# Reordering the start of a one-core RWKV-plus-MLP kernel: the columns' step ahead of zeroing, k turned ahead of r, and VectorE's early steps and four loads in another order

## The chip, the cores and the metric

The kernel runs on one core of one Trainium2 chip. A core has five engines with a queue of instructions each: TensorE (PE in the profile, with its weight loads as PEld), VectorE (DVE), ScalarE (ACT), GpSimd (POOL) and SyncE (SP). Each engine takes its queue strictly in order, and engines wait for one another with semaphores. The metric is the device time of one execution in microseconds (us); less is better. Before the change it is 168.96 us, the median of 3 runs (168.95 to 168.97).

## The reference

A linear-attention layer with a decaying state is followed by a two-layer MLP with a leaky ReLU. There are 4 batches, 8 heads, 768 tokens and a head size of 48, so the MLP sees 3072 tokens of 384 features.

```
B, H, S, D = r.shape                      # 4, 8, 768, 48
state = np.zeros((B, H, D, D))
for t in range(S):
    cur = einsum('bhd,bhe->bhde', u[None] * kt, vt)
    y[:, :, t] = einsum('bhd,bhde->bhe', rt, state + cur)
    state = w[None, :, :, None] * state + einsum('bhd,bhe->bhde', kt, vt)
x = y.transpose(0, 2, 1, 3).reshape(B * S, H * D)      # 3072 x 384
h = x @ w_in                              # 384 x 2048
out = np.maximum(0.01 * h, h) @ w_out     # 2048 x 384
```

## The kernel before

The 3072 tokens are cut into 24 stages of 128 tokens. Stage n handles batch n mod 4 and the 128-token chunk n div 4, so stages 0 to 3 are the first chunk of the four batches and carry no state; from stage 4 on a state from four stages earlier is read.

Each stage goes through the same steps, and each step has a short name. The string ORDER near the top of the file lists these names; a small scheduler walks the list, records each step on its engine, derives the waits from what is read and written, and plays the five queues. The place of a name in ORDER therefore sets the order within an engine's queue and, for TensorE, which PSUM bank a step takes; names of different engines that stand side by side do not hold one another up unless one needs the other's result. The names that matter here, with the line that issues the instructions:

- Loads, all issued by GpSimd except the first k (ScalarE's queue) and the first r and the small vectors (SyncE's queue): `k5`, `r4`, `v1` are one stage's k, r or v (L241, or L232 for stage 0); `wi0` to `wi3` are quarters of w_in (L251), `wo0` to `wo3` quarters of w_out (L255); `w8` (L706), `u8` (L707), `w` (L703) and `u` (L708) are copies of the vectors w and u.
- Constants on VectorE: `ones` (L278), `one` (L709), `qk0` (six memsets, L319), `v0z` and `v0y` (zero the gaps of v, L310), `wlz` (L322, L323), `zr` (L314, L315), `id8` (a small identity, L302), `id` (identity, L294), `tri` (mask, L298), `exps` (L306). GpSimd makes `tcol` (L268) and `trow` (L273), token numbers.
- The columns of decays: `Cw` on TensorE (L542) needs `w8`, `id8` and `zr`; `Wl` (L561) takes its logarithm on ScalarE, and `E` (four activations, L354) makes the table of decays by token with which stage 0 is scaled. `bc` on TensorE (L335) spreads w over 128 rows; `lnw` (L342), `qtab` and `ktab` (L349) make the tables for the other stages on ScalarE. `u16`, `U`, `utab` (L363, L367, L372) spread u. `wu8`, `Cu`, `C` (L359, L553, L568) make columns of w times u.
- Stage 0's operands: `c0q@` and `c0k@` cast r and k on VectorE (L438); `T0q` and `T0k` turn them on TensorE (L453); `t0q` and `t0k` scale them out of PSUM on VectorE (L466).
- Other early stages: `P1q`, `P1k` scale r and k by a table on VectorE (L390); `T1q`, `T1k` turn them on TensorE (L453); `t1q`, `t1k` copy them out on ScalarE (L471). From stage 6 a DMA turns them instead (`X6T`, L395).
- `A` multiplies the turned tiles into 128x128 scores on TensorE (L482); `M0a`, `M0b` mask one half each on VectorE (L491, from stage 4 L495). For stages 0 to 3 the diagonal comes from `X` on VectorE (product of the turned tiles, L405), `D` on TensorE (L510) and `Q` on VectorE (v scaled by it, L412). From stage 4 on it comes from `q` on VectorE (three instructions, L419, L421, L423) and `Q` on GpSimd, which writes two diagonal tiles (L430) into the buffers that `M` then fills in.
- `Y` forms the attention output on TensorE (L614 for stages 0 to 3, L621), `y` copies it to xT on ScalarE (L635). `K` forms k-times-v on TensorE (L523), `S` the next state on VectorE (L586, later L589 and L591); `W` (L576) is the table of decays for the states.
- The MLP: `G` and `J` are blocks of the first matmul (L660) and `g` and `j` their leaky ReLU on ScalarE (L671); `H` is the second matmul (L684), `h` its copy and the store (L696, L698).
- `F9` means nine matmuls of ones times ones whose result nobody reads (L288).

TensorE starts with small work that waits for loads and constants. From some 14 us on it has MLP blocks of the first stages between the attention steps, and after the first 22 us it runs to the end with next to no idle time.

Of the kernel before, what the change touches and what calls it, by code (L numbers as in the profile page):

```python
# [26 lines left out]
ORDER = """
w8 qk0 k0 v0z one r0 trow ones v0y tcol wlz r1 id8 F9 wi1 u8 zr table Cw Wl id E w bc lnw c0q@ T0q c0k@ tri u exps k1
T0k u16 wu8 Cu t0q t0k qtab P1q F6 k3 v3 U A0 ktab T1q v0 t1q X0 C D0 P1k T1k t1k F4 M0b P3k M0a T3k K3 utab X1 A1 D1
Q0 Y0 t3k P0k r3 P3q M1a T3q r2 P2q y0 k2 K0 M1b v1 Q1 W G0.1 Y1 t3q X3 wi3 A3 y1 g0.1 S3 T2q D3 G1.1 g1.1 k5 t2q r5 r4  # L30
P2k T2k wi2 S0 v2 M3b t2k Q3 G0.3 g0.3 G1.3 k4 M3a Y3 P5k A2 y3 P4q T4q v4 wi0 T5k v5 wo3 t4q g1.3 G3.1 q5 t5k Q5 G3.3
g3.3 P5q r6 wo2 X2 g3.1 M2b D2 wo1 G3.2 Q2 G0.2 g0.2 T5q t5q K2 P4k T4k M2a t4k S2 G1.2 g3.2 q4 Q4 K1 S1 Y2 A5 A4 G1.0
y2 G2.1 M5a G0.0 G2.3 M4a M5b Y5 g0.0 y5 M4b Y4 y4 G2.2 g2.2 K4 J2.4 j2.4 k6 wo0 J2.1 J2.2 g1.0 g1.2 S4 k7 P6q q6 j2.1
P6k P7k G2.0 r7 q7 X6T J2.6 j2.6 J2.3 j2.3 k8 G3.0 J2.7 j2.7 k9 r9 j2.2 J2.5 P7q g3.0 g2.3 X7T J2.0 H1 h1 r8 q8 g2.0 Q6
P9k j2.0 P8k H0 j2.5 H3 Q7 A6 P9q X9T P8q X8T v6 A7 M6a v7 M7a g2.1 H2 h2 v9 v11 v10 M6b Y6 M7b y6 Q8 q9 Y7 y7 K5 r11
K6 S6 r10 k10 S5 Q9 v8 K7 S7 h0 h3 k11 J3.0 j3.0 J3.1 j3.1 J3.2 j3.2 J3.3 j3.3 J3.4 j3.4 J3.5 j3.5 J3.6 j3.6 J3.7 j3.7
A8 A9 M8a M8b M9a M9b P10q P10k X10T P11q P11k X11T k12 r12 v12 k13 r13 v13 q10 Q10 q11 Q11 H4 h4 Y8 Y9 y8 y9 K8 K9 S8
S9 H5 h5 J4.0 j4.0 J4.1 j4.1 J4.2 j4.2 J4.3 j4.3 J4.4 j4.4 J4.5 j4.5 J4.6 j4.6 J4.7 j4.7 A10 A11 M10a M10b M11a M11b
P12q P12k X12T P13q P13k X13T k14 r14 v14 k15 r15 v15 q12 Q12 q13 Q13 H6 h6 Y10 Y11 y10 y11 K10 K11 S10 S11 H7 h7 J5.0
j5.0 J5.1 j5.1 J5.2 j5.2 J5.3 j5.3 J5.4 j5.4 J5.5 j5.5 J5.6 j5.6 J5.7 j5.7 A12 A13 M12a M12b M13a M13b P14q P14k X14T  # L40
P15q P15k X15T k16 r16 v16 k17 r17 v17 q14 Q14 q15 Q15 H8 h8 Y12 Y13 y12 y13 K12 K13 S12 S13 H9 h9 J6.0 j6.0 J6.1 j6.1
J6.2 j6.2 P16q P16k X16T P17q P17k X17T A14 A15 J6.3 j6.3 M14a M14b M15a M15b k18 r18 v18 k19 r19 v19 J6.4 j6.4 J6.5
j6.5 J6.6 j6.6 J6.7 j6.7 q16 Q16 q17 Q17 H10 h10 Y14 Y15 y14 y15 K14 K15 S14 S15 H11 h11 J7.0 j7.0 J7.1 j7.1 J7.2 j7.2
P18q P18k X18T P19q P19k X19T A16 A17 J7.3 j7.3 M16a M16b M17a M17b k20 r20 v20 k21 r21 v21 J7.4 j7.4 J7.5 j7.5 J7.6
j7.6 J7.7 j7.7 q18 Q18 q19 Q19 H12 h12 Y16 Y17 y16 y17 K16 K17 S16 S17 H13 h13 J8.0 j8.0 J8.1 j8.1 J8.2 j8.2 P20q P20k
X20T P21q P21k X21T A18 A19 J8.3 j8.3 M18a M18b M19a M19b k22 r22 v22 k23 r23 v23 J8.4 j8.4 J8.5 j8.5 J8.6 j8.6 J8.7
j8.7 q20 Q20 q21 Q21 H14 h14 Y18 Y19 y18 y19 K18 K19 S18 S19 H15 h15 J9.0 j9.0 J9.1 j9.1 J9.2 j9.2 P22q P22k X22T P23q
P23k X23T A20 A21 J9.3 j9.3 M20a M20b M21a M21b J9.4 j9.4 J9.5 j9.5 J9.6 j9.6 J9.7 j9.7 q22 Q22 q23 Q23 H16 h16 Y20 Y21
y20 y21 H17 h17 J10.0 j10.0 J10.1 j10.1 J10.2 j10.2 A22 A23 J10.3 j10.3 M22a M22b M23a M23b J10.4 j10.4 J10.5 j10.5
J10.6 j10.6 J10.7 j10.7 H18 h18 Y22 Y23 y22 y23 H19 h19 J11.0 j11.0 J11.1 j11.1 J11.2 j11.2 J11.3 j11.3 J11.4 j11.4  # L50
J11.5 j11.5 J11.6 j11.6 J11.7 j11.7 H20 h20 H21 h21 H22 h22
"""


# [750 lines left out]
```

## Time and profile before

| what | value |
|---|---|
| median of 3 runs | 168.96 us |
| the profiled execution's own time | 168.68 us |
| its span, first to last instruction | 166.8 us |
| TensorE busy | 160.2 us, 96% of the span |
| VectorE, ScalarE, GpSimd busy | 107.6, 89.0, 111.0 us |

The profile is of one execution. Its times are counted from the first instruction of the span, so some 1.8 us of the execution's own time lie outside it. In the timeline a row gives the start, the duration in us, the engine, the line, the operation and the tiles written and read; several instructions of a kind in a row are merged, and a bracket at the end gives the idle time before the row and what ended it. TensorE's matmuls overlap, so the pace of a series is read from the start of one to the start of the next.

### The profile page before, as it was taken

To read this page: it belongs to the slowest core of one execution; us is meant where nothing else is said; L and a number is where in the kernel's file an instruction comes from. 1 tells how busy PE (TensorE), PEld (TensorE's weight loads), DVE (VectorE), ACT (ScalarE), POOL (GpSimd) and SP (SyncE) were. 2 spreads that over 40 slices of the span, in tenths; PEclk is the share of its full clock that TensorE was granted. 3 is DMA by queue.
4 is the path that set the end of the run, shared out by engine and by line. 5 is a ranking of instruction groups with operands and counts; after the bars stand their busy time and mean duration, and the time that the engine had idled before them with its cause. 6 is when DMAs were issued, how large, how long until landed. Compare 5 with 4: busy or idle time off the path is not lost.

```text
span 166.8 us, 4840 instructions
## 1 busy us (share of the span) xinstructions
PE 160.2 (96%) x2076; PEld 120.6 (72%) x2076; DVE 107.6 (64%) x224; ACT 89.0 (53%) x168; POOL 111.0 (67%) x125
## 2 busy tenths in 40 slices
...
GB/s 109 156 140 157 169 193 192 171 149 173 93 168 220 113 157 130 105 108 155 105 146 118 152 127 127 156 140 140 154 51 165 12 47 51 0 47 51 35 59 96
DMA packets 101267, 20.18 MB, mean 121 GB/s; under 512 B 94459, under 2 KB 101246, under 8 KB 101246
## 3 DMA queue, kind: packets, MB, share of 16 engines
...
q10 hardware_dynamic: 1040, 0.20, 0.6%
q14 instruction: 5, 0.04, 0.1%
HBM read 20.45 MB, written 4.72 MB: 151 GB/s over the span
## 4 chain that ended last, share of the span: by engine, by line
PE 86%; POOL 7%; DMA 3%; DVE 2%; issue 0%; ACT 0%; POOLq 0%
PE ps L684 38%; PE ps L660 36%; PE ps L621 6%; DMA r_sb<-in_r_dram 3%; PE ps L482 3%; PE ps L523 2%; POOL r_sb L241 2%; POOL k_sb L241 2%; POOL v_sb L241 2%; POOL w_in_sb L251 1%; DVE prod L405 1%; DVE s_tok L423 0%; PE ps L453 0%; POOL trow L273 0%; DVE rku L421 0%
## 5 line engine op out<-in xcount | busy, mean ns | idle before, releaser
L660 PE MATMUL ps<-xT,w_in_sb 128*128 128x256 bf16 (+1 forms) x672 | 67.2, 257 | 0.0
L684 PE MATMUL ps<-w_out_sb,gT 128*128 128x384 bf16 (+2 forms) x400 | 65.6, 320 | 0.0
L671 ACT ACTIVATE gT<-ps 128x512 bf16<-128x512 f32 x96 | 56.3, 598 | 13.8 <-PE ps L660 9.7
L660 PEld LDWEIGHTS ps<-xT,w_in_sb 128*128 128x128 bf16 x672 | 57.1, 98 | 7.5 <-DVE sum_t L589 0.5
L430 POOL TENSOR_TENSOR at<-ident,s_tok 128x512 bf16<-128x512 bf16 x40 | 42.7, 1096 | 23.4 <-DVE s_tok L423 23.4
L684 PEld LDWEIGHTS ps<-w_out_sb,gT 128*128 128x128 bf16 x400 | 37.7, 98 | 22.4
L696 ACT ACTIVATE out_sb<-ps 128x384 f32<-128x384 f32 (+2 forms) x25 | 11.8, 477 | 54.5 <-PE ps L684 54.5
L495 DVE CAST_PREDICATED at<-mask,ps 128x512 bf16<-128x512 uint16 x40 | 24.9, 684 | 21.3 <-PE ps L482 21.2
L241 POOL DMA_DIRECT2D v_sb<-in_v_dram x24 | 22.1, 927 | 0.0
L241 POOL DMA_DIRECT2D k_sb<-in_k_dram x23 | 21.2, 925 | 0.0
L241 POOL DMA_DIRECT2D r_sb<-in_r_dram x23 | 21.1, 924 | 0.1
L421 DVE TENSOR_TENSOR rku<-r_sb,ku 128x384 bf16<-128x384 bf16 x20 | 13.8, 688 | 1.1 <-DMA r_sb<-in_r_dram 0.5
L589 DVE TENSOR_TENSOR sum_t<-ps,st 128x384 bf16<-128x384 f32 x16 | 8.8, 550 | 5.6 <-PE ps L523 5.6
L635 ACT ACTIVATE xT<-ps 128x384 bf16<-128x384 f32 x24 | 10.8, 490 | 2.6 <-PE ps L621 2.6
L423 DVE TENSOR_REDUCE s_tok<-rku 128x8 f32<-128x384 bf16 x20 | 11.1, 553 | 0.7
L591 DVE TENSOR_TENSOR st<-sum_t,wl 128x384 bf16<-128x384 bf16 x16 | 10.6, 664 | 0.6
L621 PE MATMUL ps<-at,v_sb 128*32 128x128 bf16 x384 | 10.8, 223 | 0.0
L390 DVE TENSOR_TENSOR qk<-k_sb,ktab 128x384 bf16<-128x384 bf16 x23 | 10.1, 444 | 1.1 <-DMA k_sb<-in_k_dram 1.1
L621 PEld LDWEIGHTS ps<-tp,st 128*32 128x32 bf16 x240 | 7.3, 96 | 3.0 <-issue 1.6
L621 PEld LDWEIGHTS ps<-at,v_sb 128*32 128x32 bf16 x384 | 8.8, 98 | 0.5 <-issue 0.2
L621 PE MATMUL ps<-tp,st 128*32 128x128 bf16 x240 | 9.1, 221 | 0.0
L390 DVE TENSOR_TENSOR qk<-r_sb,qtab 128x384 bf16<-128x384 bf16 x23 | 8.8, 386 | 0.2 <-DMA r_sb<-in_r_dram 0.2
...
## 6 DMA issues: line engine op xcount, KB each, us to landing
...
tp<-qk SPq DMA_TRANSPOSE x18, 5.3
...
```

Source lines behind the costliest of these rows:

```text
L241: add("pool", lambda: G.dma_start(dst, src), R=pace, W=[(which, n)], dma=f"{which}{n}")
L390: add("dve", lambda: V.tensor_tensor(qk[iq][:, H * half:H * half + H, 0:D], hd(src), hd(tab[:, :]), ALU.mult), R=[(name, n), "qk"[half] + ...
L421: add("dve", lambda: V.tensor_tensor(rku[i2][:, :], r_of(n), ku[i2][:, :], ALU.mult), R=[("r", n), ("ku", i2)], W=[("rku", i2)])
L423: add("dve", lambda: V.tensor_reduce(s_tok[i2][:, :], hd(rku[i2][:, :]), AX.X, ALU.add), R=[("rku", i2)], W=[("s", i2)])
L430: add("pool", lambda hh=hh, s_of=s_of: G.tensor_tensor(at[ia][:, hh, :, :], ident[:, :].unsqueeze(1).to_broadcast([128, NP, 128]), s_of.un ...
L495: add("dve", lambda: V.copy_predicated(at[n % NAT][:, hh, :, :], mask[:, :].bitcast(mybir.dt.uint16).unsqueeze(1).to_broadcast([128, NP, 1 ...
L621: last = PE.matmul(ps_y[32 * q:32 * q + 32, 128 * s:128 * s + 128], a, m, start=not whole and step == 0, stop=step == len(columns[q]) - 1)
L635: add("act", lambda: A.activation(xT[ix][:, :, 128 * slot:128 * slot + 128], ps_y[:, 0:HD].rearrange("p (s t) -> p s t", t=128), AF.Copy), ...
L660: last = PE.matmul(ps_g[:, step * f:step * f + step], w_in_sb[:, s, 128 * fb:128 * fb + 128], xT[ix][:, s, t], start=s == 0, stop=s == NSL ...
L671: add("act", lambda: A.activation(gT[ig][:, fb0:fb0 + count, t], ps_g[:, :].rearrange("p (f t) -> p f t", t=128 * width), AF.Prelu, alpha= ...
L684: last = PE.matmul(ps_o[:, 0:c1 - c0], gT[ig][:, s, 128 * slot:128 * slot + 128], w_out_sb[:, s, c0:c1], start=s == 0, stop=s == NFB - 1)
L696: add("act", lambda: A.activation(out_sb[io][:, c0:c1], ps_o[:, 0:c1 - c0], AF.Copy), R=[key], W=held)
```

## The change

Only ORDER changes; no step is altered or dropped, and the set of steps is the same but for the filler: `F9` and `F4` stay, `F6` goes, `F14`, `F7` and `F3` come (19 filler matmuls before, 37 after). From `P2k` on, the list is the same but for one name, `X2`, that moves. By engine:

- VectorE: `ones` becomes the first instruction. `id8`, `zr` and `id` move ahead of `v0z`, `v0y` and `wlz`. `c0k@` goes ahead of `c0q@`, `t0k` ahead of `t0q`. `P0k` moves from ahead of `P3q` to behind `P2q`; `M1a`, `M1b` and `Q1` move ahead of `P2q` and `P0k`. `X2` moves from behind `P5q` to ahead of `P4q`.
- TensorE: `F14` first, then `Cw`, `F9`, `T0k`, `bc`, `T0q`, `Cu`, `F7`, `A0`, `F3`, `T1q`, `D0`, `U`, `T1k`. `U` was ahead of `A0`. `K3` and `K0`, which stood around `A1` and ahead of `G0.1`, move behind `Y1`.
- ScalarE: `u16` moves behind `qtab` and `ktab`.
- SyncE: `w` is issued ahead of `u8`.
- GpSimd: the loads behind `wi1`, `k1`, `k3` were `v3 v0 r3 r2 k2 v1` and are now `v0 r3 r2 v1 k2 v3`; from `wi3` on the queue is the same.

```diff
 ORDER = """
-w8 qk0 k0 v0z one r0 trow ones v0y tcol wlz r1 id8 F9 wi1 u8 zr table Cw Wl id E w bc lnw c0q@ T0q c0k@ tri u exps k1
-T0k u16 wu8 Cu t0q t0k qtab P1q F6 k3 v3 U A0 ktab T1q v0 t1q X0 C D0 P1k T1k t1k F4 M0b P3k M0a T3k K3 utab X1 A1 D1
-Q0 Y0 t3k P0k r3 P3q M1a T3q r2 P2q y0 k2 K0 M1b v1 Q1 W G0.1 Y1 t3q X3 wi3 A3 y1 g0.1 S3 T2q D3 G1.1 g1.1 k5 t2q r5 r4
-P2k T2k wi2 S0 v2 M3b t2k Q3 G0.3 g0.3 G1.3 k4 M3a Y3 P5k A2 y3 P4q T4q v4 wi0 T5k v5 wo3 t4q g1.3 G3.1 q5 t5k Q5 G3.3
-g3.3 P5q r6 wo2 X2 g3.1 M2b D2 wo1 G3.2 Q2 G0.2 g0.2 T5q t5q K2 P4k T4k M2a t4k S2 G1.2 g3.2 q4 Q4 K1 S1 Y2 A5 A4 G1.0
...
+ones w8 qk0 k0 one r0 trow tcol id8 zr id r1 w F14 wi1 u8 v0z v0y wlz table Cw Wl E u F9 c0k@ T0k bc lnw c0q@ T0q tri
+exps k1 wu8 t0k Cu t0q qtab F7 k3 v0 r3 r2 v1 k2 v3 ktab u16 P1q A0 F3 T1q t1q X0 C D0 U P1k T1k t1k F4 M0b P3k M0a T3k
+utab X1 A1 D1 Q0 Y0 t3k P3q M1a T3q y0 M1b Q1 P2q P0k W G0.1 Y1 K0 K3 t3q X3 wi3 A3 y1 g0.1 T2q S3 D3 G1.1 g1.1 k5 t2q
+r5 r4 P2k T2k wi2 S0 v2 M3b t2k Q3 G0.3 g0.3 G1.3 k4 M3a Y3 P5k X2 A2 y3 P4q T4q v4 wi0 T5k v5 wo3 t4q g1.3 G3.1 q5 t5k
+Q5 G3.3 g3.3 P5q r6 wo2 g3.1 M2b D2 wo1 G3.2 Q2 G0.2 g0.2 T5q t5q K2 P4k T4k M2a t4k S2 G1.2 g3.2 q4 Q4 K1 S1 Y2 A5 A4
...
```

More of the change, by code (lines that the diff above doesn't have):

```diff
@@ L33 @@
[L33 to L51, printed above, removed]
+ones w8 qk0 k0 one r0 trow tcol id8 zr id r1 w F14 wi1 u8 v0z v0y wlz table Cw Wl E u F9 c0k@ T0k bc lnw c0q@ T0q tri
@@ new lines @@
+exps k1 wu8 t0k Cu t0q qtab F7 k3 v0 r3 r2 v1 k2 v3 ktab u16 P1q A0 F3 T1q t1q X0 C D0 U P1k T1k t1k F4 M0b P3k M0a T3k
+utab X1 A1 D1 Q0 Y0 t3k P3q M1a T3q y0 M1b Q1 P2q P0k W G0.1 Y1 K0 K3 t3q X3 wi3 A3 y1 g0.1 T2q S3 D3 G1.1 g1.1 k5 t2q
+r5 r4 P2k T2k wi2 S0 v2 M3b t2k Q3 G0.3 g0.3 G1.3 k4 M3a Y3 P5k X2 A2 y3 P4q T4q v4 wi0 T5k v5 wo3 t4q g1.3 G3.1 q5 t5k
+Q5 G3.3 g3.3 P5q r6 wo2 g3.1 M2b D2 wo1 G3.2 Q2 G0.2 g0.2 T5q t5q K2 P4k T4k M2a t4k S2 G1.2 g3.2 q4 Q4 K1 S1 Y2 A5 A4
+G1.0 y2 G2.1 M5a G0.0 G2.3 M4a M5b Y5 g0.0 y5 M4b Y4 y4 G2.2 g2.2 K4 J2.4 j2.4 k6 wo0 J2.1 J2.2 g1.0 g1.2 S4 k7 P6q q6
@@ new lines @@
+j2.1 P6k P7k G2.0 r7 q7 X6T J2.6 j2.6 J2.3 j2.3 k8 G3.0 J2.7 j2.7 k9 r9 j2.2 J2.5 P7q g3.0 g2.3 X7T J2.0 H1 h1 r8 q8
+g2.0 Q6 P9k j2.0 P8k H0 j2.5 H3 Q7 A6 P9q X9T P8q X8T v6 A7 M6a v7 M7a g2.1 H2 h2 v9 v11 v10 M6b Y6 M7b y6 Q8 q9 Y7 y7
+K5 r11 K6 S6 r10 k10 S5 Q9 v8 K7 S7 h0 h3 k11 J3.0 j3.0 J3.1 j3.1 J3.2 j3.2 J3.3 j3.3 J3.4 j3.4 J3.5 j3.5 J3.6 j3.6
+J3.7 j3.7 A8 A9 M8a M8b M9a M9b P10q P10k X10T P11q P11k X11T k12 r12 v12 k13 r13 v13 q10 Q10 q11 Q11 H4 h4 Y8 Y9 y8 y9
+K8 K9 S8 S9 H5 h5 J4.0 j4.0 J4.1 j4.1 J4.2 j4.2 J4.3 j4.3 J4.4 j4.4 J4.5 j4.5 J4.6 j4.6 J4.7 j4.7 A10 A11 M10a M10b
@@ new lines @@
+M11a M11b P12q P12k X12T P13q P13k X13T k14 r14 v14 k15 r15 v15 q12 Q12 q13 Q13 H6 h6 Y10 Y11 y10 y11 K10 K11 S10 S11
+H7 h7 J5.0 j5.0 J5.1 j5.1 J5.2 j5.2 J5.3 j5.3 J5.4 j5.4 J5.5 j5.5 J5.6 j5.6 J5.7 j5.7 A12 A13 M12a M12b M13a M13b P14q
+P14k X14T P15q P15k X15T k16 r16 v16 k17 r17 v17 q14 Q14 q15 Q15 H8 h8 Y12 Y13 y12 y13 K12 K13 S12 S13 H9 h9 J6.0 j6.0
+J6.1 j6.1 J6.2 j6.2 P16q P16k X16T P17q P17k X17T A14 A15 J6.3 j6.3 M14a M14b M15a M15b k18 r18 v18 k19 r19 v19 J6.4
+j6.4 J6.5 j6.5 J6.6 j6.6 J6.7 j6.7 q16 Q16 q17 Q17 H10 h10 Y14 Y15 y14 y15 K14 K15 S14 S15 H11 h11 J7.0 j7.0 J7.1 j7.1
```

8 lines of the change are left out of this document (added).

## The prediction

> **What bounds the kernel now.** I read first where TensorE is idle, because it is the busiest engine. The view by stretches has start:end, length, then busy time (and instructions) of TensorE, its weight loads, VectorE, ScalarE and GpSimd, the granted clock, the DMA share and GB/s.
>
> ```profile
> 13.30:21.60 8.30, 7.67 (x153) 6.49 (x151) 7.66 (x17) 7.03 (x16) 7.62 (x10) 1.00 1.96 170
> 21.60:164.50 142.90, 142.85 (x1823) 106.92 (x1823) 88.75 (x171) 74.46 (x139) 90.75 (x96) 1.00 1.19 117
> ```
>
> From 21.60 us on TensorE is busy for 142.85 of 142.90 us. The change leaves that work as it is, so the end moves by as much as the point moves from which TensorE runs without a pause. That point is set by the chain of work that ended last (start, duration, what):
>
> ```profile
> 12.77 5.69 DMA r_sb<-in_r_dram
> ...
> 18.48 0.04 DVE qk L390
> ...
> 20.09 0.27 DVE qk L390
> 20.35 1.20 DVE prod L405
> ...
> 21.60 0.25 PE ps L510 x4
> ```
>
> The load of r for stage 4 (`r4`) lands, VectorE scales it (`P4q`), does `q5`, `P5q` and `X2` (L405), and only then can `D2` start. The timeline round that place:
>
> ```profile
> 17.07 1.08 ACT L471 ACTIVATE tp<-ps 128x512 bf16<-128x512 f32 x2
> 17.97 0.35 DVE L390 TENSOR_TENSOR qk<-k_sb,ktab 128x384 bf16<-128x384 bf16 x1
> 18.48 0.36 DVE L390 TENSOR_TENSOR qk<-r_sb,qtab 128x384 bf16<-128x384 bf16 x1 [0.16 <-DMA r_sb<-in_r_dram]
> 19.05 0.62 PE L453 MATMUL ps<-ident,qk 128*128 128x128 bf16 x8
> 19.51 1.50 PE L660 MATMUL ps<-xT,w_in_sb 128*128 128x128 bf16 x24
> 19.54 0.55 DVE L423 TENSOR_REDUCE s_tok<-rku 128x8 f32<-128x384 bf16 x1
> 20.17 2.27 POOL L430 TENSOR_TENSOR at<-ident,s_tok 128x512 bf16<-128x512 bf16 x2 [0.68 <-DVE s_tok L423]
> 20.27 1.27 DVE L405 TENSOR_TENSOR prod<-tp 128x512 bf16<-128x512 bf16 x1
> 21.60 0.25 PE L510 MATMUL ps<-wu,prod 128*128 128x2 bf16 x4 [0.58 <-DVE prod L405]
> ```
>
> The operands of `X2` were copied out by ScalarE at 18.15 (17.07 + 1.08), two microseconds before it ran. It ran from 20.27 to 21.54, beside GpSimd's two tiles. TensorE meanwhile had issued its 24 matmuls: they start 0.056 us apart ((1.50 - 0.22) / 23, the last one taking 0.22 by the second row below), so the next could have started at 19.51 + 24 x 0.056 = 20.85. The pause there is worth 21.60 - 20.85 = 0.75 us.
>
> A second thing to read is the pace of one kind of matmul, the turning ones, before and after some 13.1 us (count, then min/median/max ns, first and last start):
>
> ```profile
> L453 PE MATMUL ps<-ident,qk x14: 268/314/314, 9.0 to 13.0; 128*128 128x128 bf16 x14
> ...
> L453 PE MATMUL ps<-ident,qk x26: 219/219/314, 13.1 to 23.6; 128*128 128x128 bf16 x26
> ```
>
> The same matmul takes 314 ns up to 13.0 us and 219 later, while the clock column says 1.00 throughout; in series they start 0.107 us apart before (nine fillers, 1.14 us, in the rows below: (1.14 - 0.29) / 8) and 0.056 after. TensorE thus starts slow and is let go at about 13.3 us.
>
> **The change part by part.** The rows for the start:
>
> ```profile
> 0.83 0.87 DVE L319 MEMSET qk<- 128x128 uint32 x6 [0.83 <-PEq L790]
> 2.09 0.17 DVE L278 MEMSET ones<- 128x128 bf16 x1
> 2.31 1.14 PE L288 MATMUL ps<-ones 128*128 128x128 bf16 x9 [2.31 <-DVE ones L278]
> 2.47 1.12 DVE L310 MEMSET v_sb<- 128x1280 uint32 x1 [0.21 <-issue]
> 3.73 0.40 DVE L302 TENSOR_SCALAR ident<-trow,tcol 8x8 f32<-8x8 f32 x1
> 4.24 0.38 PE L542 MATMUL ps<-ident,w_head 8*64 8x4 f32 x4 [0.78 <-DVE w_head L315]
> 4.49 0.71 DVE L438 CAST raw<-r_f 128x384 bf16<-128x384 f32 x1 [0.20 <-DMA r_f<-in_r_dram]
> 5.11 1.01 PE L335 MATMUL ps<-w_row,one_row 1*128 1x192 f32 x4 [0.50 <-DMA w_row<-in_w_dram]
> 6.05 1.03 PE L453 MATMUL ps<-ident,raw 128*128 128x128 bf16 x8
> 6.77 1.29 DVE L466 TENSOR_TENSOR tp<-ps,turned 128x512 bf16<-128x512 f32 x2 [0.79 <-PE ps L453]
> 8.03 0.49 PE L367 MATMUL ps<-u_row,ones 1*128 1x384 bf16 x1
> 10.82 0.41 DVE L405 TENSOR_TENSOR prod<-tp 128x512 bf16<-128x512 bf16 x1
> 11.62 0.55 DVE L390 TENSOR_TENSOR qk<-k_f,ktab 128x384 bf16<-128x384 f32 x1
> 13.82 0.54 DVE L412 TENSOR_TENSOR vs<-v_sb,ps 128x384 bf16<-128x384 bf16 x1
> 15.36 0.40 PE L453 MATMUL ps<-ident,qk 128*128 128x128 bf16 x4
> ```
>
> *Columns ahead of zeroing.* `ones`, the six memsets and `one` end at about 0.83 + 0.17 + 0.87 + 0.17 = 2.0; `id8`, `zr` and `id` took from 3.73 to 4.24 together, so `Cw` starts near 2.7 instead of 4.24, and the decay table is done 1.5 us sooner. That is hidden, though: the 1.12 us of zeroing now runs behind it, the casts still start at about 4.3 (before, r's cast waited for its load until 4.49), and `T0q` stands behind `bc` on TensorE. `T0k` starts at 4.7 and takes 0.43 (four at 0.107), `bc` holds the queue for 0.94 (5.11 to 6.05), so `T0q` starts at 6.05 as before. `bc` started at 5.11 on the landing of `w`; issued ahead of `u8` it lands sooner and isn't late.
>
> *k ahead of r.* Before, both scalings of stage 0 stood behind 6.77 and ended at 8.06. Now `t0k` is done in the gap ahead of 6.77 (VectorE was idle for 0.79 there) and `t0q` ends at 7.46: 0.6 us gained on VectorE. TensorE gives half of it back, since `F3` (3 x 0.107) and `U` (0.43: 8.03 to the next start at 8.46) now stand between `A0` and `T1k`. `X1` therefore starts at 10.5 instead of 10.82. If `c0k@` takes the 0.71 of the first cast instead of the 0.34 of the second, 0.35 of this is lost again.
>
> *Steps of stages 0 and 1 ahead.* `P0k` and `P2q` (0.55 and, like other L390 rows, 0.35; less an overlap of 0.08 each, 0.74) leave the way of `M1a`, `M1b`, `Q1`: `Q1` starts at 12.8 instead of 13.82. They come back behind it, so `X3` is only 0.5 early. `K0` and `K3` (four matmuls each, 0.17 at the fast pace) now stand behind `Y1` and ahead of `A3`, and `S3` waits for `K3`: the series up to `T2q`, which started at 15.36, is 0.2 early (15.14), and by `P5k` the lead is 0.1 us (17.86 instead of 17.97). Lower bound nothing, upper 0.9 if TensorE's faster pace comes sooner; I take 0.1, since VectorE has the same steps to do by then.
>
> *Loads.* From `wi3` on GpSimd's queue is unchanged and waits for nothing, so `r4` lands at about 18.46 again. `v1` lands earlier; `v3` takes the last place, where `v1` was (its user `Q1` started at 13.82), and its new first user `K3` stands at about 14.6: free.
>
> *X2 ahead of P4q.* `X2` starts behind `P5k` at 18.15 and takes its undisturbed time:
>
> ```profile
> L405 DVE TENSOR_TENSOR prod<-tp x4: 414/422/1268, 8.2 to 20.3; 128x512 bf16<-128x512 bf16 x4
> ```
>
> The 1268 is `X2` beside GpSimd's tiles, the 414 to 422 are the other three. So it ends at 18.55; `P4q` starts at 18.47 (the overlap of neighbours is 0.08) and ends at 18.82, as with `r4` alone. Without the 0.1 us of lead it would be 18.95. Behind it wait `q5`, GpSimd's tiles and `T4q`; none is later than before.
>
> **The sum.** `T4q` starts at 18.9 to 18.95 instead of 19.05, TensorE goes on for the 1.80 us from 19.05 to 20.85, and `D2` starts at 20.73 instead of 21.60: 0.87 us, of which 0.75 is the pause and 0.12 the lead. Does it last? The next limit is the diagonal of stage 4:
>
> ```profile
> 23.33 1.51 POOL L255 DMA_DIRECT2D w_out_sb<-in_moe_w_out_dram x2
> 25.53 2.04 POOL L430 TENSOR_TENSOR at<-ident,s_tok 128x512 bf16<-128x512 bf16 x2 [0.68 <-DVE s_tok L423]
> 25.82 2.67 DVE L495 CAST_PREDICATED at<-mask,ps 128x512 bf16<-128x512 uint16 x4
> 28.84 0.23 PE L621 MATMUL ps<-tp,st 128*32 128x128 bf16 x4
> ```
>
> GpSimd was free at 24.84 (23.33 + 1.51) and waited for `q4` until 25.53; with `q4` 0.87 earlier it starts at 24.84 and ends at 26.88. The last mask ended 0.92 behind GpSimd's tiles (28.49 against 27.57), now at 27.80, and `Y4` is due at 28.84 - 0.87 = 27.97. It holds by 0.17 us. Off the profiled execution's own 168.68 (1.8 outside its 166.8 span) this gives 167.81; the median runs stand 0.28 higher, so the forecast is 168.96 - 0.87 = 168.09, about **168.1 us**.
>
> [...]
>
> **The rivals.** *Only X2 counts* (the first part doesn't do what it is for). If `T1k` or the first casts come late, the lead is gone, `P4q` ends at 19.1 behind `X2`, `T4q` starts at 19.25, `D2` at 21.05: 0.55 gained, 168.4. For it: `U` and `F3` in the way; against it: 1.0 us at `Q1`.
>
> *TensorE is let go earlier*, by the fillers from 1.05 us on. Then `P4q` waits for `r4` alone, `D2` starts at 20.68; were `r4` to land 0.4 sooner as well, 167.7. Against it, TensorE was without a pause for long and still slow (start:end, length, its busy time):
>
> ```profile
> 6.50:9.90 3.40, 3.40 (x37) 1.00 2.52 144
> 9.90:13.30 3.40, 3.40 (x51) 1.00 2.26 133
> ```
>
> *The other side: TensorE is let go later.* `K3` and `K0` no longer fill the gaps ahead of `A1` and `G0.1`, and `Y0` waits some 0.35 for `Q0`, so the stretch ahead of 13.3 has pauses that it did not have. The first release took 7.2 us of work without a pause (6.05 to 13.3); take half of that, 3.6 us, as the delay. Then `G0.1`, `Y1`, `K0`, `K3` and `A3`, 1.9 us at the fast pace from 13.0 on, take 3.3 to 3.7 (0.107 against 0.056), `T2q` starts at 16.35 to 16.75, and with the 3.69 from `T2q` to `T4q` as before (15.36 to 19.05) `T4q` at 20.05 to 20.45 and `D2` at 21.85 to 22.25: 0.25 to 0.65 later, 169.2 to 169.6. The delay decides once it passes some 2 us, since a microsecond at the slow pace costs about half of one. [...]
>
> *GpSimd's tiles take the pause over.* If `q4` gains nothing, the last mask ends at 28.49 and `Y4` can't start before 28.53, 0.3 ahead of 28.84: 168.7.
>
> **How the numbers follow.** The forecast has 0.53, only `X2` 0.14, earlier 0.06, GpSimd's tiles 0.08, later 0.19. 0.2% is 0.34 us, about what a measurement of this kernel can tell from no change. The first three are faster by more: 0.73. Same is 0.08 for the tiles and 0.06 of the late pace (up to 0.34 of its 0.25 to 0.65, and shorter delays): 0.14; slower is the other 0.13. The forecast's own range is 167.8 to 168.5 (0.35 of a slow cast, 0.3 of an earlier `r4`). The range for all, 167.6 to 169.25, leaves out most of the late pace and little else.
>
> **What would show it.** Right: `Cw` (L542) near 2.7; the second scaling (L466) done by 7.5; L412 of stage 1 near 12.8; the third L405 row near 18.1 with 0.42; L453 of stage 4 near 18.9 and `D2` (L510) near 20.7 with no idle time ahead of it. Wrong: turning matmuls of 314 ns behind 14 us, `r4` landing away from 18.46, or a new pause ahead of `Y4`.

## The result, and the profile after

| | before | after |
|---|---|---|
| median of the runs | 168.95 us (168.81 to 168.97, 4 runs) | 170.41 us (170.33 to 171.33, 4 runs) |
| ratio, with its 95% interval | | 1.0106 (1.0082 to 1.0131) |
| the profiled execution's own time | 168.68 us | 170.46 us |
| its span | 166.8 us | 168.7 us |

The changed kernel is slower by 1.46 us, or 1.1%; the forecast was 0.87 us faster. Beside the experiments (e1 to e4, e5 to e8, e9 to e12, e13 to e15) the kernel before took 168.32 to 171.09 us, with medians of 169.03, 168.88, 168.96 and 169.07: the three first runs, which agreed within 0.02 us, had shown far too little spread. The ratios leave out eight executions in a slower state (two of e4, three of e8, two of e13, one of the kernel before), the medians keep them, and e4's profile is of one of them.

The view by stretches of the kernel after, with the same columns as the one in the prediction, cut where TensorE's pauses lie:

```profile
15.07:21.88 6.81, 6.76 (x144) 5.88 (x142) 5.82 (x15) 4.90 (x10) 5.29 (x7) 1.00 2.08 166
21.88:47.96 26.08, 26.08 (x365) 20.65 (x363) 17.89 (x33) 13.62 (x27) 23.92 (x27) 1.00 1.70 155
47.96:49.84 1.88, 0.33 (x3) 0.00 (x1) 1.88 (x5) 0.49 (x1) 1.88 (x3) 1.00 0.78 142
49.84:166.31 116.47, 116.44 (x1460) 86.45 (x1460) 68.65 (x136) 61.22 (x112) 65.93 (x69) 1.00 1.07 107
```

The pause at 20.8 is gone: TensorE is busy for 6.76 of the 6.81 us up to 21.88. A new pause of 1.55 us stands at 47.96 (1.88 less 0.33). TensorE ends at 166.31 instead of 164.48, and the 1.83 us come from two places: `D2` starts 0.28 later (21.88 against 21.60), and the new pause is 1.55.

**The first place.** The timeline of the kernel after round `D2`:

```profile
18.05 1.08 ACT L471 ACTIVATE tp<-ps 128x512 bf16<-128x512 f32 x2
19.00 0.35 DVE L390 TENSOR_TENSOR qk<-k_sb,ktab 128x384 bf16<-128x384 bf16 x1
19.26 0.42 DVE L405 TENSOR_TENSOR prod<-tp 128x512 bf16<-128x512 bf16 x1
19.60 0.35 DVE L390 TENSOR_TENSOR qk<-r_sb,qtab 128x384 bf16<-128x384 bf16 x1
20.08 0.62 PE L453 MATMUL ps<-ident,qk 128*128 128x128 bf16 x8
20.54 1.50 PE L660 MATMUL ps<-xT,w_in_sb 128*128 128x128 bf16 x24
21.88 0.24 PE L510 MATMUL ps<-wu,prod 128*128 128x2 bf16 x4
```

`X2` (L405) takes 0.42 us, and `D2` (L510) has no idle time ahead of it. That part did what it is for. But `P5k` starts at 19.00, where it was 17.97 before. The lateness is from the start, as the timeline there shows, first of the kernel before, then of the kernel after:

```profile
13.54 0.84 PE L660 MATMUL ps<-xT,w_in_sb 128*128 128x128 bf16 x12
...
15.11 0.55 DVE L586 TENSOR_TENSOR st<-ps,wl 128x384 bf16<-128x384 f32 x1
```
```profile
13.65 1.44 PE L660 MATMUL ps<-xT,w_in_sb 128*128 128x128 bf16 x12 [0.15 <-ACT xT L635]
15.58 0.51 PE L523 MATMUL ps<-v_sb,qk 128*128 128x96 bf16 x8
16.13 0.56 DVE L586 TENSOR_TENSOR st<-ps,wl 128x384 bf16<-128x384 f32 x1 [0.92 <-PE ps L523]
16.36 0.40 PE L453 MATMUL ps<-ident,qk 128*128 128x128 bf16 x4
16.69 0.83 PE L660 MATMUL ps<-xT,w_in_sb 128*128 128x128 bf16 x12
```

In the kernel after, twelve matmuls of L660 take 1.44 us from 13.65 on and 0.83 from 16.69 on: TensorE was let go between them. The trace's own record of the clock puts that at 15.07. For the kernel before it is at 13.32, and the twelve at 13.54 (`G0.1`) take 0.84 there. `K0` and `K3` (L523), now behind that slow work, hold up `S3` (L586), and VectorE is idle for 0.92 us ahead of it. `T2q` starts at 16.36, before at 15.36.

**The second place.** First VectorE and GpSimd of the kernel before:

```profile
39.88 0.65 DVE L421 TENSOR_TENSOR rku<-r_sb,ku 128x384 bf16<-128x384 bf16 x1 [0.47 <-DMA r_sb<-in_r_dram]
42.43 1.46 DVE L390 TENSOR_TENSOR qk<-r_sb,qtab 128x384 bf16<-128x384 bf16 x2
45.17 2.48 DVE L495 CAST_PREDICATED at<-mask,ps 128x512 bf16<-128x512 uint16 x4 [1.28 <-PE ps L482]
...
44.69 2.10 POOL L430 TENSOR_TENSOR at<-ident,s_tok 128x512 bf16<-128x512 bf16 x2
```

Then the same work of the kernel after, with `Y6` on TensorE:

```profile
42.49 0.36 DVE L421 TENSOR_TENSOR rku<-r_sb,ku 128x384 bf16<-128x384 bf16 x1 [2.22 <-DMA r_sb<-in_r_dram]
44.74 3.25 DVE L390 TENSOR_TENSOR qk<-r_sb,qtab 128x384 bf16<-128x384 bf16 x2
47.91 2.47 DVE L495 CAST_PREDICATED at<-mask,ps 128x512 bf16<-128x512 uint16 x4
...
45.54 2.23 POOL L430 TENSOR_TENSOR at<-ident,s_tok 128x512 bf16<-128x512 bf16 x2
...
49.84 0.24 PE L621 MATMUL ps<-tp,st 128*32 128x128 bf16 x4 [1.55 <-DVE at L495]
```

The second instruction of `q8` (L421) waits 2.22 us for the load of r for stage 8 (`r8`). `P9q` and `P8q` (L390) therefore run into GpSimd's two tiles `Q8` (L430), which start at 45.54: the pair takes 3.25 us instead of 1.46. Before, the pair had ended at 43.89, ahead of the tiles at 44.69. (`P9q` alone took 1.19 us there, without any tile, while GpSimd issued loads; it takes 2.13 now, and `P8q` 1.20 instead of 0.34.) The masks of stages 6 and 7 (L495) then start at 47.91 instead of 45.17, though TensorE has their scores by 45.6 (45.3 before), and `Y6` waits for them. No engine was given more work: a wait of 2 us moved two short instructions under two long ones.

### The profile page after: what moved, and what is told of

It is laid out like the page before. It is cut to its first block, busy times and chain, and to the rows that moved or that the text cites. A ratio compares the mean times of both kernels' runs of the same rounds, so it can differ in the third digit from the quotient of the medians.

```text
span 168.7 us, 4876 instructions
## 1 busy us (share of the span) xinstructions
PE 162.9 (97%) x2094; PEld 123.1 (73%) x2094; DVE 106.7 (63%) x224; ACT 89.5 (53%) x168; POOL 111.4 (66%) x125
## 4 chain that ended last, share of the span: by engine, by line
PE 91%; DVE 6%; issue 1%; ACT 0%; DVEq 0%
PE ps L660 37%; PE ps L684 36%; PE ps L621 6%; PE ps L482 4%; PE ps L523 3%; PE ps L453 2%; DVE at L495 1%; PE ps L288 1%; DVE qk L390 1%; DVE v_sb L310 1%; PE ps L614 1%; DVE at L491 1%; DVE st L586 1%; PE ps L335 1%; DVE qk L319 0%
## 5 line engine op out<-in xcount | busy, mean ns | idle before, releaser
L660 PE MATMUL ps<-xT,w_in_sb 128*128 128x256 bf16 (+1 forms) x672 | 67.5, 259 | 0.2 <-ACT xT L635 0.2
L671 ACT ACTIVATE gT<-ps 128x512 bf16<-128x512 f32 x96 | 56.3, 598 | 13.2 <-PE ps L660 8.9
L660 PEld LDWEIGHTS ps<-xT,w_in_sb 128*128 128x128 bf16 x672 | 57.8, 99 | 7.4 <-issue 0.4
L430 POOL TENSOR_TENSOR at<-ident,s_tok 128x512 bf16<-128x512 bf16 x40 | 42.7, 1095 | 24.8 <-DVE s_tok L423 24.8
L495 DVE CAST_PREDICATED at<-mask,ps 128x512 bf16<-128x512 uint16 x40 | 24.9, 684 | 20.3 <-PE ps L482 20.2
L421 DVE TENSOR_TENSOR rku<-r_sb,ku 128x384 bf16<-128x384 bf16 x20 | 13.5, 674 | 3.1 <-DMA r_sb<-in_r_dram 2.5
L390 DVE TENSOR_TENSOR qk<-k_sb,ktab 128x384 bf16<-128x384 bf16 x23 | 9.5, 415 | 3.2 <-DMA k_sb<-in_k_dram 3.2
L621 PE MATMUL ps<-at,v_sb 128*32 128x128 bf16 x384 | 10.9, 223 | 0.0
L621 PE MATMUL ps<-tp,st 128*32 128x128 bf16 x240 | 9.2, 221 | 1.6 <-DVE at L495 1.6
L621 PEld LDWEIGHTS ps<-tp,st 128*32 128x32 bf16 x240 | 7.2, 96 | 4.8 <-DVE at L495 2.1
L390 DVE TENSOR_TENSOR qk<-r_sb,qtab 128x384 bf16<-128x384 bf16 x23 | 10.6, 465 | 0.0
L591 DVE TENSOR_TENSOR st<-sum_t,wl 128x384 bf16<-128x384 bf16 x16 | 10.0, 625 | 0.6
L621 PEld LDWEIGHTS ps<-at,v_sb 128*32 128x32 bf16 x384 | 8.8, 98 | 0.5 <-issue 0.2
```

The lines of the kernel that those rows point to most:

```text
L390: add("dve", lambda: V.tensor_tensor(qk[iq][:, H * half:H * half + H, 0:D], hd(src), hd(tab[:, :]), ALU.mult), R=[(name, n), "qk"[half] + ...
L421: add("dve", lambda: V.tensor_tensor(rku[i2][:, :], r_of(n), ku[i2][:, :], ALU.mult), R=[("r", n), ("ku", i2)], W=[("rku", i2)])
L430: add("pool", lambda hh=hh, s_of=s_of: G.tensor_tensor(at[ia][:, hh, :, :], ident[:, :].unsqueeze(1).to_broadcast([128, NP, 128]), s_of.un ...
L495: add("dve", lambda: V.copy_predicated(at[n % NAT][:, hh, :, :], mask[:, :].bitcast(mybir.dt.uint16).unsqueeze(1).to_broadcast([128, NP, 1 ...
L621: last = PE.matmul(ps_y[32 * q:32 * q + 32, 128 * s:128 * s + 128], a, m, start=not whole and step == 0, stop=step == len(columns[q]) - 1)
L660: last = PE.matmul(ps_g[:, step * f:step * f + step], w_in_sb[:, s, 128 * fb:128 * fb + 128], xT[ix][:, s, t], start=s == 0, stop=s == NSL ...
```

## The experiments

All were timed beside the kernel before, several runs each; ratios are to it, with 95% intervals. Each edit is one of ORDER. Two questions were asked: which part of the change makes the loss, and by which way.

### Only X2, and all but X2

Kernel before with `X2` moved (e1), kernel after with `X2` moved back (e2):

```diff
-... Y3 P5k A2 y3 P4q ... r6 wo2 X2 g3.1 ...
+... Y3 P5k X2 A2 y3 P4q ... r6 wo2 g3.1 ...
```

> Kernel before with X2 alone ahead of P4q. Theory A (the loss has two steps: TensorE is let go at 15.1 instead of 13.3 us, and later P9q and P8q fall under GpSimd's tiles of stage 8): neither step is in this edit, so D2 starts at 20.9 to 21.1 instead of 21.6, no pause ahead of Y6, 168.2 to 168.5 us. Rival R1 (moving X2 is what shifts VectorE against GpSimd and makes the pause ahead of Y6): a pause of 1 us or more there, 169.3 or more.

> Changed kernel with X2 back behind P5q. Theory A: the 0.75 us that X2 gave is lost at D2 (22.4 to 22.7 if TensorE is let go as late as in the changed kernel) and the later pause stays in some size, 170.4 to 171.3 us. Rival R1: without X2's move there is no pause ahead of Y6, 168.9 to 169.8.

e1: 168.88 us, ratio 0.9988 (0.9956 to 1.002); `D2` at 21.17 instead of 21.60. e2: 170.44 us, ratio 1.0086 (1.0058 to 1.0114); `D2` at 22.98. So `X2` isn't the cause of the loss: without it the loss stays. Its own gain of 0.43 us at `D2` can't be told from none in the time, and the 168.2 to 168.5 expected of e1 is missed. e1's profile shows one way in which it is lost: TensorE is idle for 0.30 us ahead of 31.26, taken up below. e2's time is as expected, but its profile has no pause ahead of `Y6`: `P8q` ends at 45.84 and the tiles start at 46.09. The loss of that execution is `D2`, 1.38 late, and 1.20 us of idle time at 31.34.

### q8 out of the way, and GpSimd's tiles out of the way

Kernel after with `q8` behind `X8T` (e3), and with `Q8` behind `k10` (e4):

```diff
-... h1 r8 q8 g2.0 Q6 ... P9q X9T P8q X8T v6 ...
+... h1 r8 g2.0 Q6 ... P9q X9T P8q X8T q8 v6 ...
```
```diff
-... M7b y6 Q8 q9 Y7 y7 ... r10 k10 S5 Q9 ...
+... M7b y6 q9 Y7 y7 ... r10 k10 Q8 S5 Q9 ...
```

> Changed kernel with VectorE's q8 (which waited for r8 until 42.5 us) behind P9k, P8k, P9q and P8q. Theory A: these four are done ahead of GpSimd's tiles of stage 8, the masks of stages 6 and 7 come in time, the 1.55 us pause ahead of Y6 is gone: 168.8 to 169.1 us. Rival R2 (VectorE is held by GpSimd's load issues as well, and the pause stays): 170 or more.

> Changed kernel with GpSimd's tiles of stage 8 behind the loads r11, r10 and k10; q8 still waits for r8. Theory A (it takes both, the late r8 and the tiles): P9q and P8q take 0.35 us each or up to 1.2, the pause ahead of Y6 is under 0.4: 168.8 to 169.3 us. Rival R3 (the wait for r8 alone makes the masks late): the pause stays above 1 us, 170.2 to 170.6.

e3: 169.90 us, ratio 1.004 (1.0006 to 1.0074). `r8` lands at 42.26, about as late as in the kernel after, but `P8q` starts at 42.28, and the pause ahead of `Y6` is gone. So it is by way of `q8` that the late load makes the second place. The time is 1 us higher than expected. The profiled execution was late for other reasons: TensorE was let go at 16.45, `D2` started at 22.43, and TensorE was idle for 0.70 us ahead of 31.46. e4: 170.27 us, ratio 1.0039 (1.0001 to 1.0077). Its ratio is as low as e3's, which would fit that the tiles are needed for the second place too. But the expected 168.8 to 169.3 is missed, and its profile (an execution of 173.13 us) tells nothing: TensorE was idle for 2.08 us ahead of 32.85, so that it was late itself, and `r8` happened to land at 40.47.

### The changed kernel again, and K3 at its old place

The kernel after, unchanged (e5); with `v3` and `K3` back in front (e6); and that with `q8` moved as in e3 (e7):

```diff
-... F7 k3 v0 ... k2 v3 ktab ... M0a T3k utab X1 A1 ... Y1 K0 K3 t3q ...
+... F7 k3 v3 v0 ... k2 ktab ... M0a T3k K3 utab X1 A1 ... Y1 K0 t3q ...
```

> The changed kernel once more, unaltered, for a second profile and more times. Theory A: TensorE let go at 15 to 16.6 us, S3 (the state of stage 3, waiting for K3) at 16.0 or later, D2 at 21.8 or later, masks of stages 6 and 7 ending at 49.5 or later; 170.2 to 170.9 us. Rival C (the first profile was an unlucky one): release near 13, D2 below 21.2, 168.5 to 169.3.

> Changed kernel with K3 back ahead of A1 (and its load v3 back behind k3). Theory K (S3 waited 0.92 us for K3, which stood behind Y1 on a slow TensorE, and VectorE was late from there on): S3 starts at 15.2 to 15.3 instead of 16.13, P4q at 18.6 to 19.0, D2 at 20.8 to 21.4; the later pause ahead of Y6 stays, 169.6 to 170.3 us. Rival G (only the late release counts): P4q stays at 19.4 or later and D2 at 21.8 or later, 170.2 or more.

> K3 and v3 back as in e6, and q8 behind P8q as in e3. Theory A with K: both steps of the loss are gone, D2 at 20.8 to 21.4, no pause ahead of Y6, 168.3 to 168.8 us. Rival (something else in the start is late): 169.3 or more.

e5: 170.43 us, ratio 1.0102 (1.0075 to 1.0128). Let go at 15.83, `D2` at 22.35, `r8` landed at 42.62, `P8q` at 47.01, `Y6` at 50.05: both places again, in another execution, though of the wait for the masks only 0.43 us shows at `Y6`, because TensorE had lost 0.71 us ahead of 31.37. e6: 169.76 us, ratio 1.0041 (1.0022 to 1.0059). `S3` starts at 15.27, as was expected of it, but `D2` at 22.55 against an expected 20.8 to 21.4: TensorE was let go at 17.60, the latest so far, and the early `S3` was worth nothing at `D2`. What this profile lacks is the second place, though `q8` stands where it stood: `r8` lands at 41.33, and `P8q` ends at 45.13, ahead of the tiles at 45.89. One profile can't tell whether that is by the edit or by chance. e7: 169.20 us, ratio 1.0027 (1.0004 to 1.0049), let go at 17.83; the 168.3 to 168.8 expected is missed. `K3`'s place is thus not the cause of the late `D2` by the way of `S3`; what is left, by elimination, is the time of TensorE's release.

### Filling TensorE's stretches, and taking the fillers out

Kernel after with fillers `F2` behind `A1` and `F5` behind `T3q` (e8), that with `q8` moved as in e3 (e10), and that with `U` behind `Y1` and `utab` behind `y1` (e11). Kernel before without `F6` and `F4` (e9); kernel before with `X2` and `q8` moved (e12):

```diff
-... X1 A1 D1 ... M1a T3q y0 M1b ...
+... X1 A1 F2 D1 ... M1a T3q F5 y0 M1b ...
```
```diff
-... C D0 U P1k ... T3k utab X1 ... G0.1 Y1 K0 ... A3 y1 g0.1 ...
+... C D0 P1k ... T3k X1 ... G0.1 Y1 U K0 ... A3 y1 utab g0.1 ...
```
```diff
-... qtab P1q F6 k3 ... T1k t1k F4 M0b ...
+... qtab P1q k3 ... T1k t1k M0b ...
```

> Changed kernel with two fillers behind A1 and five behind T3q, where TensorE waits. Theory G (an emptier stretch delays the release): release at 15.1 or earlier, T2q at 16.4 or earlier, D2 at 21.3 to 21.9, 169.8 to 170.3 us. Theory K: the release may move, but S3 still waits for K3 until 15.5 or later and the time stays within 0.3 of the changed kernel, 170.2 to 170.7.

> Kernel before without its fillers F6 and F4 (F9 stays). Theory H (TensorE is let go at the end of a stretch of 3.41 us, at a phase that differs from run to run, in which matmuls weighted by the part of the 128x128 array that they use fill at least some 0.75 of the time): without F4 no stretch that ends ahead of 13.7 us reaches 0.75 (with it from 11.5 on), so the release falls between 13.7 and 17.1 and the median rises to 169.2 to 169.9 us. Rival (fillers don't matter, TensorE is let go when the MLP starts at 13.5): release 13.5 or a little later, 168.8 to 169.1.

> Changed kernel with the fillers of e8 in its two gaps and q8 behind P8q as in e3. Theory A with H: release between 12.9 and 16.3, masks of stages 6 and 7 no longer late, no pause ahead of Y6: 168.6 to 169.2 us, under both e3 and e8. Rival (the two steps are one, and curing one cures the other): as e8, 169.5 or more.

> As e10, and U (a matmul that uses one row of the array for 0.43 us) with utab behind Y1. Theory H: T1k starts 0.3 sooner, stretches reach 0.75 from about 11.5 us on, release between 11.5 and 15, D2 at 20.8 to 21.6: 168.2 to 168.8 us, under the kernel before. Rival (VectorE sets the start in any case): as e10 within 0.2.

> Kernel before with X2 ahead of P4q and q8 behind P8q. Theory A: D2 as in e1 (20.8 to 21.3), release between 11.5 and 15, no late masks: 168.3 to 168.8 us, the same or up to 0.4 under the kernel before. Rival R1 (X2's move always costs later what it gains): 168.9 to 169.2.

e8: 169.64 us, ratio 1.0025 (0.9998 to 1.0053), a little under the 169.8 to 170.3 expected; in its profile `D2` is at 22.09, no earlier than in the kernel after, and `Y6` waits only 0.17 us. e10: 169.16 us, 1.002 (0.9993 to 1.0046), as expected. e11: 169.12 us, 1.001 (0.9986 to 1.0035), where 168.2 to 168.8 was expected; the rival, within 0.2 of e10, is what came, so the place of `U` shows nothing in the median. e12: 169.12 us, 1.0011 (0.999 to 1.0031), where 168.3 to 168.8 was expected and its rival had 168.9 to 169.2. In the profiles of e1 and e12 TensorE gains 0.43 and 0.23 us at `D2` and is idle for 0.30 and 0.38 us near 31; whether moving `X2` always costs later what it gains stays open. e9: 168.89 us, 0.9999 (0.9983 to 1.0015), where 169.2 to 169.9 was expected; the time is its rival's.

The profiles tell more than these medians. e11's execution was let go at 10.54, and it is the fastest of all in the experiments, 167.82 us. Its timeline on TensorE:

```profile
13.07 0.83 PE L660 MATMUL ps<-xT,w_in_sb 128*128 128x128 bf16 x12
...
15.38 0.40 PE L453 MATMUL ps<-ident,qk 128*128 128x128 bf16 x4
...
20.89 0.24 PE L510 MATMUL ps<-wu,prod 128*128 128x2 bf16 x4
```

With an early release the twelve matmuls of `G0.1` take 0.83 us, `T2q` starts at 15.38, and `D2` starts at 20.89, near the 20.73 of the forecast. e9 is the reverse, the kernel before with a late release. Its trace has no record of the clock, but twelve matmuls still take 1.48 us from 14.02 on, so the rival's release at 13.5 is not what happened:

```profile
14.02 1.48 PE L660 MATMUL ps<-xT,w_in_sb 128*128 128x128 bf16 x12
...
16.82 0.40 PE L453 MATMUL ps<-ident,qk 128*128 128x128 bf16 x4
...
20.32 0.62 PE L453 MATMUL ps<-ident,qk 128*128 128x128 bf16 x8
20.78 1.50 PE L660 MATMUL ps<-xT,w_in_sb 128*128 128x128 bf16 x24
22.12 0.24 PE L510 MATMUL ps<-wu,prod 128*128 128x2 bf16 x4
```

`T2q` is 1.46 us late, but `D2` only 0.52: the pause of 0.75 ahead of it is gone, though `X2` stands where it stood. In the kernel before that pause was also the slack that took up a late start. That may be why e9 loses nothing in the median; the profiled execution, 169.17 us, still carries the 0.52.

### The start alone, both, and r8 alone

Kernel after with `U` and `utab` moved as in e11, `F7` for `F4`, and `F5` behind `T3q` (e13); that with `q8` moved (e14); and the kernel after with only `r8` moved ahead of `k9` and `r9` (e15):

```diff
-... t1k F4 M0b ...
+... t1k F7 M0b ...
```
```diff
-... J2.7 j2.7 k9 r9 j2.2 ... H1 h1 r8 q8 ...
+... J2.7 j2.7 r8 k9 r9 j2.2 ... H1 h1 q8 ...
```

> The changed kernel, with U and utab put behind Y1, F4 made F7 and five more fillers behind T3q; q8 stays where it was. Start theory (the clock is released late since no 3.41 us stretch ahead of 13 us holds enough work on the whole array): stretches that end from 10.3 to 12.5 and behind 13.2 now hold a share of 0.75 or more, so the clock is released at 10.3 to 14.0 in about three executions of four, D2 starts at 20.8 to 21.7 and the median is 168.4 to 169.1. It also says that the pause ahead of Y6 goes with the late start, so 0.5 or less of it is left. Rival (the two losses have nothing to do with one another): D2 as above, but q8 waits for r8 until 42 and the pause of 1.5 ahead of Y6 stays, median 169.3 to 169.9. Rival (the new order of VectorE's steps is itself slow): no gain over the changed kernel, 170.2 to 170.6.

> The kernel of e13 with q8 moved behind X8T. If both losses are as told, this has neither: 168.0 to 168.6, no pause ahead of Y6, P8q ahead of GpSimd's tiles. If the clock's release decides alone, it is within 0.2 of e13. If the stall behind matmul 473 is what makes the executions differ, its median is no better than that of e11 (169.1).

> The changed kernel with the load of r for stage 8 issued ahead of those of k and r for stage 9 (some 1.9 us sooner on GpSimd's queue); all else as in the changed kernel. If q8's wait for r8 is the start of the second loss: r8 lands at 39 to 40.5, q8 goes on without a wait, P8q ends ahead of GpSimd's two tiles (45.5), no pause ahead of Y6, median 169.0 to 169.9 as in e3. If r8 lands late because the whole of the transfers is late (41 or more whatever its place), the wait and the pause stay and the time is 170.2 to 170.6. If k9 or r9 come late in its place, P9k or P9q waits.

e13: 169.18 us, ratio 1.0001 (0.9971 to 1.003). Its median is 0.11 us above that of the kernel before beside it, over times from 168.18 to 171.31, so next to nothing of the loss is left, with VectorE's new order and `q8`'s place unchanged: the new order by itself doesn't cost. The pause ahead of `Y6` is gone from its profile too, but only just: `q8` still waits 1.84 us for `r8`, and `P8q` starts at 45.27, 0.08 ahead of the tiles. In this execution the release was at 14.53 and `D2` at 22.07, later than the kernel after's 21.88, so the 20.8 to 21.7 that was expected isn't shown by it; the median just misses both ranges. e14: 169.27 us, 1.0007 (0.9979 to 1.0036), so moving `q8` adds nothing that the time can show once the start is filled. The 168.0 to 168.6 expected are missed; both other readings given there, within 0.2 of e13 and no better than e11, fit. Its profiled execution (169.98 us) was let go early, at 12.88, had `D2` at 21.61 and no pause ahead of `Y6`, and lost the time in two other pauses of TensorE, 0.84 us ahead of 24.45, where it waits for ScalarE (L471), and 0.37 ahead of 30.78.

e15: 169.86 us, ratio 1.0038 (1.0009 to 1.0067), as expected. VectorE and GpSimd of this kernel, and `Y6`:

```profile
40.97 1.08 DVE L421 TENSOR_TENSOR rku<-r_sb,ku 128x384 bf16<-128x384 bf16 x1
...
43.96 1.46 DVE L390 TENSOR_TENSOR qk<-r_sb,qtab 128x384 bf16<-128x384 bf16 x2
46.53 2.48 DVE L495 CAST_PREDICATED at<-mask,ps 128x512 bf16<-128x512 uint16 x4 [1.11 <-PE ps L482]
...
46.22 2.10 POOL L430 TENSOR_TENSOR at<-ident,s_tok 128x512 bf16<-128x512 bf16 x2
...
49.28 0.24 PE L621 MATMUL ps<-tp,st 128*32 128x128 bf16 x4
```

`r8` landed at 39.77, `q8` goes on without a wait, the pair of L390 takes 1.46 us ahead of the tiles, the masks wait for TensorE and not the other way round, and `Y6` has no pause. That is so in an execution that was let go at 18.01 and had `D2` at 22.87. So the late landing of `r8` starts the second loss, and lateness alone doesn't. Taking the second place away, by either way (e3, e15), leaves a ratio of 1.004 of the 1.0102: of the loss of about 1%, some 0.6% is the second place and 0.4% the first. With intervals of 0.3% to either side that split is rough.

The second place is a race, and it isn't lost in every execution. From the landing of `r8` to the start of the first tile of `Q8` there are 3.14, 3.13 and 3.19 us in the profiles of the kernel after, e5 and e8, where `Y6` waits 1.55, 0.43 and 0.17 us. There are 3.53, 4.05 and 4.56 us in e13, e2 and e6, with `q8` at the same place, and 4.90 in the kernel before, where it doesn't wait. Filling the start (e13) takes the loss away in the median, but one profile doesn't show by which of the two places.

No kernel here is faster than the kernel before beyond its interval; the best two ratios are e1 and e9, both the kernel before with one small edit.

### What lets TensorE go

The release lies between 10.54 and 18.01 us in the fifteen profiles that have it on record (e2 and e9 don't), and differs between executions of one kernel (15.07 and 15.83 for the kernel after). From the release to the next throttling the record has 153.60 us in nine profiles, 150.19 in e6, e7 and e15, 157.01 in e11 and e14 and 17.07 in e4, which are 45, 44, 46 and 5 times 3.413; the three longest lie 3.41 apart. That suggests a grid of 3.413 us whose place changes from run to run. So I cut each trace backwards from its release in such stretches and weighed each matmul by the part of the array that it uses: its time at the slow pace, times rows / 128, times columns / 128. A matmul on 128 rows and 32 columns counts a quarter, one on a single row next to nothing.

```
profile    release  share of the stretch  share of the one  T2q    D2     own time
                    that ended in it      ahead of it
e11        10.54    0.79                  0.38              15.38  20.89  167.82
e14        12.88    0.78                  0.66              16.03  21.61  169.98
before     13.32    0.81                  0.64              15.36  21.60  168.68
e12        13.95    0.76                  0.60              15.91  21.37  168.74
e1         13.96    0.76                  0.66              15.77  21.17  168.86
e10        14.03    0.77                  0.68              16.14  21.66  168.53
e13        14.53    0.80                  0.75              16.55  22.07  169.44
after      15.07    0.78                  0.69              16.36  21.88  170.46
e8         15.25    0.91                  0.72              16.57  22.09  169.30
e5         15.83    0.81                  0.55              16.83  22.35  170.66
e4         16.36    0.82                  0.69              16.94  22.46  173.13
e3         16.45    0.84                  0.74              16.91  22.43  170.06
e6         17.60    0.81                  0.74              16.94  22.55  169.83
e7         17.83    0.81                  0.73              16.94  22.66  169.96
e15        18.01    0.81                  0.71              17.18  22.87  170.16
```

In all fifteen, the stretch that ended in the release has 0.76 or more, and the one ahead of it, which didn't release, 0.75 or less. Other weights don't part the two: by rows alone the lowest share that released is 0.79 and the highest that didn't 1.11 (matmuls on 32 columns run side by side: in the kernel before the first four of L621 start within 0.01 us, at 12.32), by columns alone 0.78 and 0.97, by the time in which any matmul streams 0.74 and 0.82. Busy time in the profile doesn't part them either; the view by stretches of the kernel before and then of the kernel after:

```profile
6.49:9.91 3.42, 3.42 (x37) 2.48 (x36) 3.05 (x8) 2.14 (x6) 3.42 (x5) 1.00 2.51 144
9.91:13.32 3.41, 3.41 (x51) 2.62 (x49) 3.41 (x10) 2.06 (x5) 3.41 (x5) 1.00 2.26 134
```
```profile
8.24:11.66 3.42, 3.42 (x37) 2.61 (x34) 2.74 (x7) 1.98 (x5) 3.42 (x5) 1.00 2.66 140
11.66:15.07 3.41, 3.24 (x43) 2.53 (x42) 3.15 (x8) 1.83 (x5) 3.41 (x5) 1.00 1.58 152
```

The stretch 8.24 to 11.66 is full by time and didn't release; 11.66 to 15.07 has less time and did. By array share the first has 0.69: turning matmuls 0.375, fillers 0.219, the scores of `A1`, on 48 of 128 rows, 0.094, and `U`, one row, 0.001 for its 0.32 us. In the kernel before, the stretch 9.91 to 13.32 has 0.81, of which `K3` and `K0` are 0.107. With a stretch slid over the trace instead of the grid's place, the kernel before has 0.75 or more from an end at 11.5 on, and the kernel after, but for 0.2 us at 13.2, only from one at 15.0 on. Then the release should fall at 11.5 to 15 before and, but for a grid that ends near 13.2, at 15 to 18.4 after, and it did in the three profiles of these two kernels.

The edits bear it out by groups. The changed order without more fillers (after, e3 to e7, e15) was let go at 15.07 to 18.01, that with fillers added (e8, e10, e11, e13, e14) at 10.54 to 15.25, and the kernel before and its variants with `F6` and `F4` (before, e1, e12) at 13.32 to 13.96. The rule itself is inferred from these traces; no run changed the share of one stretch and nothing else.

## Why the prediction was wrong

**Right.** `Cw` starts at 2.65 (near 2.7 was predicted), the second scaling is done at 7.46 (by 7.5), `X2` takes 0.42, `D2` has no idle time ahead of it, and the limit at `Y4` holds (no pause there). `r4` lands at 18.91 instead of 18.46, in time for `P4q` at 19.60, though it would have been late for the `P4q` at 18.47 of the forecast. `P4k` fell beside the second tile of `Q5`: it starts at 22.63, takes 0.96 us, where most rows of L390 take 0.35, and ends at 23.59, behind that tile's end at 23.38. It came without cost to TensorE, which is busy for 26.08 of the 26.08 us from 21.88 on.

**Too early by a little.** `X1` starts at 10.96 (10.5 was predicted) and `Q1` at 13.24 (12.8), since VectorE waits 0.56 us for the load of k for stage 1 ahead of `P1k`. The term "0.6 us gained on VectorE" was spent on that wait. It was not decisive: `Q1` is still 0.58 earlier than before.

**The step that failed first: "the series up to `T2q` ... is 0.2 early (15.14)".** It was 16.36, 1.22 later than said, and `P5k`, for which a lead of 0.1 us and at worst none was taken, came 1.03 late (19.00). The rival "TensorE is let go later" had this place and very nearly these numbers: it gave `T2q` at 16.35 to 16.75 and `D2` at 21.85 to 22.25, and 16.36 and 21.88 were measured. I gave it a chance of 0.19. Its delay was taken as 3.6 us from "7.2 us of work without a pause"; measured were 1.75 us in one execution and 2.5 in the other. That its places came out all the same is in part luck: it had `G0.1` start at 13.0, and it started at 13.65. What misled me was the view of busy time: 6.5 to 9.9 and 9.9 to 13.3 both read 3.40 of 3.40, so I took both stretches as full, and had no measure of how much the work mattered that moved out of the second. By array share these two were 0.64 and 0.81. By the rule above only the second counted, and the change left the stretch of 8.24 to 11.66 with 0.69. That stretch was busy by time, for 3.42 of its 3.42 us, and TensorE wasn't let go at its end.

**The step that cost most: "Does it last? The next limit is the diagonal of stage 4".** I checked that limit, at 28 us, and took everything behind it as a plain shift, from "TensorE is busy for 142.85 of 142.90 us". No rival had a pause later than `Y4`. The pause of 1.55 us ahead of `Y6` is most of the 1.83. The rows for it were in the profile before: `q8` already waited 0.47 us for `r8`, and `P8q` ended 0.80 us ahead of GpSimd's tiles. A landing 2.6 us later (42.40 against 39.79), with tiles only 0.85 later, broke that.

**Right, but not a gain that the time can show.** "Only `X2` counts" said 168.4 for `X2` alone. `D2` moved by 0.43 of the 0.55 that it said, but e1 reads 168.88. The pause of 0.75 us that the forecast removes was no fixed loss: e9 shows that a late start uses it up.

**Open.** Why `r8` lands 2.6 us later after the change, while its issue is 0.47 later (34.01 against 33.54). The load has sixteen landing records; in the kernel after, eleven lie at 40.24 or earlier and the other five at 42.11 to 42.40. It is the last of six loads of k and r issued without a break (29.68 to 34.95), but it was that before too; in e15, where `r9` is the last, `r9` lands at 42.70 and `r8` at 39.77. Whether moving the tiles away helps is open too: e4's ratio suggests it, and no profile shows it.
